# A recurrence and a routed expert layer: loads of two steps at a time

## The chip, the cores and the metric

The kernel runs on one core of one Trainium2 chip. Its engines are TensorE (PE, with its weight load PEld), VectorE (DVE), ScalarE (ACT), GpSimd (POOL) and SyncE (SP), which issues nearly all transfers. The metric is the device time of one execution in microseconds. The kernel before takes 266.89 us, the median of 3 runs (266.56 to 266.95).

## The reference

Attention with a decaying state over 4 batches, 8 heads, 768 positions and heads of 48, and behind it a layer of 8 experts, each row going to one of them.

```python
for t in range(S):
    kt, vt, rt = (k[:, :, t], v[:, :, t], r[:, :, t])
    cur = np.einsum('bhd,bhe->bhde', u[None] * kt, vt)
    y[:, :, t] = np.einsum('bhd,bhde->bhe', rt, state + cur)
    state = w[None, :, :, None] * state + np.einsum('bhd,bhe->bhde', kt, vt)
...
x = y.transpose(0, 2, 1, 3).reshape(B * S, H * D)
do_compute = x @ w_skip > 0
e_idx = argmax(x @ w_gate);  gate_w = softmax(x @ w_gate)[e_idx]
out = x + gate_w * (relu(x @ w1[e_idx]) @ w2[e_idx])   # rows with do_compute, else out = x
```

All is float32. The experts' weights are split into two parts on the chip, a high and a low one, and each product is made of three.

## The kernel before

**Stage 1, the recurrence (to about 113 us).** The 768 positions are cut into 12 steps of 64 (`NSTEP`), and two batches are handled together, so there are 24 steps in all (`NT`, two runs of 12). For step n the kernel loads one block `dm` with r and k (128 partitions, 4 KB each: two heads' 48 channels in rows 0 to 47 and 64 to 111; the other 32 rows are zeros in memory, loaded with the rest) and one block `vz` with v (positions in the partitions; two batches in two halves, each loaded by its own transfer of 64 rows; the rest of the tile is set to zero once, L323). Then

- `prep_r` (DVE, L418 and L426, with ACT L412) multiplies r by powers of the decay into `rd`; `prep_k` (POOL, L436; DVE for step 0) does k into `kd`.
- `scores` (PE, L448) multiplies `kd` by `rd` into `ps_p`; `mask_scores` (DVE, L469, L470) copies the valid part into `am`.
- `turn_k` (PE L461, ACT L463) transposes `kd`; `state` (PE, L481) multiplies it by v.
- `within` (PE, L510: `am` by v) and `across` (PE, L534: `rd` by the state so far) give the output in `ps_y`; `evac` (ACT, L545) copies it to `xt`, and SP stores it (L563, two transfers, three for steps 4 to 7).
- Every four steps the gate's scores are made and routed (L605, L622, the lines of `route`).

The loop at L902 runs n from 0 to 22. Its iteration n makes `scores(n+1)`, `turn_k(n+2)`, `prep_k(n+3)`, `prep_r(n+3)`, `state(n+1)` and `within(n+1)`, ends with the store of step n+1, and on SP issues `load_dm(n+5)`, `load_v(n+4)` and, in 15 of the iterations, a piece of the weights (`raw`, L110, 256 KB). The written order is the order on each engine: nothing is scheduled. SP's transfers stand in one queue; each waits besides its data for the transfer eight places before it to have landed. `dm` has four buffers, and so has `vz`; `load_dm(n+5)` writes into the buffer of step n+1, when `rd` and `kd` of that step are made.

**Stage 2 (to about 131 us)** finishes the routing, gathers the first rows (POOL, L128) and starts the first expert with the rows transposed; its tiles `xhl`, `h` (tag `dm`) take buffers of the pool `ld`. **Stage 3** runs the other experts, PE-bound matmuls on gathered rows, weights loaded by SP and split by ACT, DVE and POOL.

Of the kernel before, what the change touches and what calls it, by code (L numbers as in the profile page):

```python
# [9 lines left out]
F32 = mybir.dt.float32  # L10
# [10 lines left out]
B, H, S, D = 4, 8, 768, 48  # L21
N, DM, E, F = B * S, H * D, 8, 1024
P = 128
C = 64
# [4 lines left out]
NHP = H // 2  # L29
NT = NPAIR * NSTEP  # L30
# [8 lines left out]
DR = P  # L39
ADV = NB * NHP  # L40
BIG = 4 * N
NVK = 4
GB = 4
BH = 2
NDM = 4
# [16 lines left out]
def tile_wkv_moe(  # L62
# [11 lines left out]
    nc = tc.nc  # L74
# [168 lines left out]
        mix(y, q)  # L243


    lctx = ExitStack()
    ld = lctx.enter_context(tc.tile_pool(name="ld", bufs=NDM, side="right"))
    vctx = ExitStack()
    vp = vctx.enter_context(tc.tile_pool(name="vp", bufs=1, side="right"))
    with ExitStack() as actx:  # L250
# [17 lines left out]
        ub_sb = tab.tile([DR, NHP], F32, name="ub_sb")  # L268
        nc.scalar.dma_start(out=ub_sb, in_=ub)

        loaded = {}
        vz = [vp.tile([P, 2, 2, NHP, D], F32, name=f"vz{j}") for j in range(NVK)]

        def load_dm(n):
            pr, i = divmod(n, NSTEP)
            d = ld.tile([P, 2, NHP, 2, C], F32, tag="dm", name=f"dm{n}", bufs=NDM)
            nc.sync.dma_start(out=d, in_=dm[pr, i])
            loaded[n] = [d[:DR], None]

        def load_v(n):  # L280
            pr, i = divmod(n, NSTEP)
            t = vz[n % NVK]
            for q in range(2):
                half = slice(q * C, (q + 1) * C)
                nc.sync.dma_start(out=t[half, q], in_=tok[pr, i, half])
            loaded[n][1] = t

        load_dm(0)
        load_dm(1)
        load_v(0)  # L290
        load_dm(2)
        load_v(1)
        load_dm(3)
        load_v(2)
        load_v(3)
        wgp = tab.tile([P, NCC, 2, C // 2], F32, name="wgp")
        pick = tab.tile([P, 2, NB, E + 1], F32, name="pick")

# [21 lines left out]
        eye = lower("eye", ALU.is_equal)  # L320
        for t in vz:
            for q in range(2):
                nc.gpsimd.memset(t[(1 - q) * C : (2 - q) * C, q], 0.0)  # L323

        w_d = tab.tile([DR, NSUB, 2, NHP, C], F32, name="w_d")

# [85 lines left out]
                nc.scalar.mul(rd[:, :, 1], rd[:, :, 0], uw[:, hp : hp + 1])  # L412

        def prep_r(n, parts=(0, 1)):
            d = loaded[n][0]
            if 0 in parts:
                rds[n] = wk.tile([DR, NHP, 2, 2, C], F32, tag="rd", name=f"rd{n}", bufs=4)
                nc.vector.tensor_tensor(  # L418
                    rds[n][:, :, :, 0],
                    d[:, 0],  # L420
                    w_d[:, n % NSUB, 0][:, :, None].to_broadcast([DR, NHP, 2, C]),
                    ALU.mult,
                )
            if 1 in parts:
                rd = rds[n]
                nc.vector.tensor_tensor(  # L426
                    rd[:, :BH, :, 1],
                    rd[:, :BH, :, 0],
                    (uw if n < 3 else uw_p)[:, :BH, None, None].to_broadcast([DR, BH, 2, C]),
                    ALU.mult,  # L430
                )

        def prep_k(n, eng=None):
            d = loaded[n][0]
            kds[n] = wk.tile([DR, NHP, 2, C], F32, tag="kd", name=f"kd{n}", bufs=4)
            (eng or nc.gpsimd).tensor_tensor(  # L436
                kds[n],
                d[:, 1],
                w_d[:, n % NSUB, 1][:, :, None].to_broadcast([DR, NHP, 2, C]),
                ALU.mult,  # L440
            )
# [28 lines left out]
            nc.vector.copy_predicated(shape(am[n % 2]), eye, p[:, :, 1])  # L470

        def state(n):
            t = loaded[n][1]
            i, sub = n % NSTEP, n % NSUB
            if i == NSTEP - 1:
                return
            kt = kts.pop(n)
            s, nxt = ps_s[:, : 2 * NHP * D].rearrange("p (q f) -> p q f", q=2), sblk[(n + 1) % 2]
            for hp in range(NHP):
                for a in range(2):  # L480
                    nc.tensor.matmul(  # L481
                        s[a * C : (a + 1) * C, :, hp * D : (hp + 1) * D],
                        kt[:, hp, a, :],
                        t[:, :, a, hp, :],
                        start=i == 0 and hp == 0,
                        stop=True,
                        skip_group_check=True,
                    )
            if sub < NSUB - 1:
                nc.scalar.copy(nxt, s)  # L490
                return
            heads = lambda t: t.rearrange("p q (h e) -> p q h e", h=NHP)
            nc.vector.tensor_tensor(
                heads(nxt), heads(s), wh_sb[:, None, :, None].to_broadcast([P, NB, NHP, D]), ALU.mult
            )
            return lambda: nc.scalar.copy(s, nxt)
# [5 lines left out]
        def place_y(a, c):  # L502
            return ps_y[c * C : (c + 1) * C, a, : NHP * D].rearrange("p (q g e) -> p q g e", q=NB, g=NHP // 2)

        def within(n, behind=None):
            t = loaded[n][1]
            for g in range(NHP // 2):
                for a, c in FOUR:
                    hp = 2 * g + (a ^ c)
                    ins = nc.tensor.matmul(  # L510
                        place_y(a, c)[:, :, g, :],
                        am[n % 2][:, a, hp * C : (hp + 1) * C],
                        t[:, :, a, hp, :],
                        start=g == 0 and n % NSTEP == 0,
                        stop=True,
                        skip_group_check=True,
                    )
                    if behind is not None:
                        tc.add_manual_dep(
                            ins.ins,  # L520
                            behind.name,
                            mybir.DependencyInfo(mybir.DependencyClass.Sync, mybir.DependencyReason.DATA),
                            reason="other row tiles write these banks",
                        )
                        behind = None
# [320 lines left out]
            return banks[kind][(used[kind] - 1) % len(banks[kind])]  # L846

        def scratch(name, shape, dt, tag):
            return (ld if tag == "dm" else scr[0]).tile(
                [P] + shape, dt, tag=tag, name=name, bufs=NDM if tag == "dm" else 3  # L850
            )

        scr = []
# [14 lines left out]
        def piece(j, split=False):  # L868
            e, j = divmod(j, NPC)
            if split:  # L870
                split_piece(e, j, nc.gpsimd)
            else:
                load_piece(e, j)

        setup = setup_routes()
        prep_r(0)
        bonus(0, BH)
        prep_k(0, nc.vector)
# [14 lines left out]
        warm(1)  # L893
        within(0)
        evac(0)
        load_v(4)
        nc.sync.dma_start(out=wgp, in_=wgq)
        prep_r(2)
        bonus(2, BH)
        prep_k(2)  # L900
        grow(3)
        for n in range(NT - 1):  # L902
            if n + 5 < NT:
                load_dm(n + 5)
            if n + 4 < NT and n:
                load_v(n + 4)
            if n in LOADS:
                piece(LOADS.index(n))
            scores(n + 1)
# [37 lines left out]
        done = NPC  # L947
        piece(len(LOADS))
        vctx.close()
        scr.append(lctx.enter_context(tc.tile_pool(name="scr", bufs=3, side="right", reuse_waits="tile")))  # L950
        first = begin(0, "dm")

# [378 lines left out]
```

## Time and profile before

| | |
|---|---|
| median of the runs | 266.89 us (266.56 to 266.95) |
| profiled execution, whole | 264.4 us |
| its span | 262.6 us |
| granted TensorE clock | 0.996 |
| PE busy | 247.9 us, 94% |
| DVE, ACT, POOL busy | 181.0, 140.5, 131.7 us |
| moved by transfers | 53.92 MB, mean 205 GB/s |

The span is what the profiler saw from the first to the last instruction; around it the execution needs 1.8 us more. The runs without a profile lie 2.5 us above the profiled execution. PE's busy time is matmuls in a pipeline with ends that are modelled, so it tells where PE had nothing to do and not how full it was. A wait in the profile is put down to the one of several releasers that came last.

### The profile page before, as it was taken

The page shows a single profiled execution, that of the slowest core. Times are in us where ns is not written, and L with a number is a line of the kernel's source. Part 1 is how long each engine was busy: PE and PEld are TensorE (multiplying, and loading weights), DVE is VectorE, ACT ScalarE, POOL GpSimd, SP SyncE. Part 2 cuts the span into 40 slices and gives each one's busy share as a digit, 9 for nine tenths or more (in the row PEclk, how much of TensorE's full clock was granted, in tenths as well). Part 3 has the DMA queues.
Part 4 walks back from the last instruction along what each step waited for, and adds up shares of the span by engine and source line. Part 5 has one row for each costly group of instructions (what it writes and reads, how often), then busy time and mean ns, then how long its engine had stood idle before and what let it go on. Part 6 is the DMA issues. An engine that isn't in the chain of part 4 may idle for free.

```text
span 262.6 us, 8820 instructions
## 1 busy us (share of the span) xinstructions
PE 247.9 (94%) x3594; PEld 228.5 (87%) x3594; DVE 181.0 (69%) x366; ACT 140.5 (53%) x314; POOL 131.7 (50%) x130
## 2 busy tenths in 40 slices
PE   7799999989999999998999999999999999999990
PEld 2698898977988989877899899999999999999980
DVE  7976667786888989674567997979277484692210
ACT  2555667757865767434658628358085381660200
POOL 8656424547555365405689818454535355345011
PEclk9999999999999999999999999999999999999998
DMA  6978779899987897767798896877648475001000
GB/s 195 268 225 253 216 223 272 264 255 269 273 256 226 257 245 243 204 189 243 222 308 261 267 325 206 261 238 244 215 143 255 141 228 199 20 1 47 1 34 21
DMA packets 31137, 53.92 MB, mean 205 GB/s; under 512 B 4603, under 2 KB 14471, under 8 KB 31088
## 3 DMA queue, kind: packets, MB, share of 16 engines
q1 hardware_dynamic: 28896, 48.09, 60.5%
q0 software_dynamic: 2048, 5.18, 6.5%
q8 instruction: 30, 0.49, 0.8%
q14 instruction: 19, 0.16, 0.2%
q10 hardware_dynamic: 144, 0.00, 0.0%
HBM read 45.46 MB, written 8.39 MB: 205 GB/s over the span
## 4 chain that ended last, share of the span: by engine, by line
PE 82%; DMA 5%; DVE 4%; ACT 2%; POOL 2%; issue 1%; SPq 0%; POOLq 0%; DVEq 0%; ACTq 0%
PE ps_y L170 11%; PE ps_p L170 10%; PE ps_p L448 7%; PE ps_y L510 6%; PE ps_s L481 6%; PE ps_p L160 5%; PE ps_r L160 5%; PE ps_l L160 5%; PE ps_y L160 5%; PE ps_l L461 4%; PE ps_y L534 3%; PE ps_t L577 3%; PE ps_l L605 2%; POOL kd L436 2%; DMA xg<-out_dram,gid 2%; DMA raw<-in_w_dram 2%
## 5 line engine op out<-in xcount | busy, mean ns | idle before, releaser
L116 POOL TENSOR_TENSOR lo<-raw,hi 128x512 fp32r<-128x512 f32 x40 | 52.8, 1324 | 39.8 <-ACT hi L115 39.6
L115 ACT CAST hi<-raw 128x512 fp32r<-128x512 f32 x96 | 54.7, 623 | 1.9 <-DMA raw<-in_w_dram 1.7
L116 DVE TENSOR_TENSOR lo<-raw,hi 128x512 fp32r<-128x512 f32 x56 | 51.1, 936 | 2.5 <-ACT hi L115 2.3
L436 POOL TENSOR_TENSOR kd<-dm,w_d 128x512 f32<-128x512 f32 x23 | 33.6, 1460 | 31.5 <-DMA dm<-in_dm_dram 14.5
L178 POOL DMA_INDIRECT out_dram<-xg,sid x16 | 17.4, 1084 | 37.6 <-DVE xg L175 29.1
L469 DVE COPY_PREDICATED am<-below,ps_p 128x512 f32<-128x512 int8 x24 | 17.7, 736 | 13.4 <-PE ps_p L448 13.2
L448 PE MATMUL ps_p<-rd,kd 64*64 64x128 f32 x768 | 26.7, 276 | 0.0
L128 POOL DMA_INDIRECT xg<-out_dram,gid x16 | 18.5, 1153 | 15.3 <-DMA raw<-in_w_dram 10.6
L164 ACT ACTIVATE hh<-ps_p 128x464 fp32r<-128x464 f32 x7 | 3.9, 559 | 37.7 <-PE ps_p L160 35.7
L418 DVE TENSOR_TENSOR rd<-dm,w_d 128x512 f32<-128x512 f32 x24 | 21.9, 912 | 3.1 <-DMA dm<-in_dm_dram 3.1
L448 PEld LDWEIGHTS ps_p<-rd,kd 64*64 64x64 f32 x768 | 20.9, 133 | 3.3 <-issue 1.2
L510 PE MATMUL ps_y<-vz,am 128*64 128x96 f32 x384 | 20.3, 248 | 0.9 <-DVE am L470 0.7
L463 ACT COPY kt<-ps_l 128x512 f32<-128x512 f32 x22 | 12.9, 585 | 14.2 <-PE ps_l L461 13.9
L412 ACT ACTIVATE rd<-rd,uw 128x128 f32<-128x128 f32 x50 | 17.2, 394 | 6.0 <-DVE rd L418 5.6
L170 PE MATMUL ps_p<-hi,hh 128*128 128x384 f32 x56 | 19.4, 347 | 0.0
L170 PE MATMUL ps_p<-hi,hl 128*128 128x384 f32 x56 | 19.0, 340 | 0.4 <-DVE hl L165 0.4
L481 PE MATMUL ps_s<-vz,kt 128*64 128x96 f32 x352 | 19.4, 253 | 0.0
L170 PE MATMUL ps_y<-hi,hh 128*104 128x384 f32 x56 | 18.9, 338 | 0.0
L510 PEld LDWEIGHTS ps_y<-vz,am 128*64 128x64 f32 x384 | 17.2, 137 | 1.9 <-DVE am L470 1.1
L170 PE MATMUL ps_y<-hi,hl 128*104 128x384 f32 x56 | 18.9, 337 | 0.0
L170 PE MATMUL ps_y<-lo,hh 128*104 128x384 f32 x56 | 18.9, 337 | 0.0
L170 PE MATMUL ps_p<-lo,hh 128*128 128x384 f32 x56 | 18.8, 336 | 0.0
(252 smaller groups left out, 653.1 us busy)
## 6 DMA issues: line engine op xcount, KB each, us to landing
raw<-in_w_dram SPq DMA_DIRECT2D x96, 256.0 KB, 4.0
dm<-in_dm_dram SPq DMA_DIRECT2D x24, 512.0 KB, 5.4
vz<-in_tok_dram SPq DMA_DIRECT2D x48, 96.0 KB, 4.8
out_dram<-xt SPq DMA_DIRECT2D x48, 96.0 KB, 4.1
out_dram<-xt SPq DMA_DIRECT2D x4, 192.0 KB, 4.3
xg<-out_dram,gid POOLq DMA_INDIRECT x16, 4.8
out_dram<-xg,sid POOLq DMA_INDIRECT x16, 3.7
wgp<-in_wgq_dram SPq DMA_DIRECT2D x1, 96.0 KB, 2.1
```

The source lines that it names most:

```text
L115: nc.scalar.copy(hi, t)
L116: eng.tensor_tensor(lo, t, hi.bitcast(F32), ALU.subtract)
L128: ins = nc.gpsimd.indirect_dma_start(out=xg[:m], out_offset=None, in_=out[0:rows], in_offset=bass.IndirectOffsetOnAxis(ap=gid[:m, q : q + ...
L160: nc.tensor.matmul(ph, a[:, c, fs], b[:, c, :], start=(k == 0), stop=(k == 3 * NCC - 1))
L170: nc.tensor.matmul(py, a, b[:, f, :], start=(k == 0), stop=(k == 3 * NFC - 1))
L178: ins = nc.gpsimd.indirect_dma_start(out=out, out_offset=bass.IndirectOffsetOnAxis(ap=sid[: listed(q), q : q + 1], axis=0), in_=xs.pop(q)[ ...
L418: nc.vector.tensor_tensor(rds[n][:, :, :, 0], d[:, 0], w_d[:, n % NSUB, 0][:, :, None].to_broadcast([DR, NHP, 2, C]), ALU.mult,)
L436: (eng or nc.gpsimd).tensor_tensor(kds[n], d[:, 1], w_d[:, n % NSUB, 1][:, :, None].to_broadcast([DR, NHP, 2, C]), ALU.mult,)
L448: nc.tensor.matmul(ps_p[q * C : (q + 1) * C, a, 2 * hp * C : 2 * (hp + 1) * C], kd[h, hp, q, :], rd[h, hp, q].rearrange("p s c -> p (s c)" ...
L469: nc.vector.copy_predicated(shape(am[n % 2]), below, p[:, :, 0])
L481: nc.tensor.matmul(s[a * C : (a + 1) * C, :, hp * D : (hp + 1) * D], kt[:, hp, a, :], t[:, :, a, hp, :], start=i == 0 and hp == 0, stop=Tr ...
L510: ins = nc.tensor.matmul(place_y(a, c)[:, :, g, :], am[n % 2][:, a, hp * C : (hp + 1) * C], t[:, :, a, hp, :], start=g == 0 and n % NSTEP ...
```

## The change

`dm` lives in two lasting tiles of two steps each, `vz` too. Steps 0 to 3 load all 128 rows, one step at a time, step 0 by two transfers (r, then k). From step 4 on, `load_dm` is called in every second iteration and loads two steps by two transfers, one of rows 0 to 47 and one of rows 64 to 111; the zeros of the first loads stay in the other rows. `load_v` loads two steps by two transfers, one for each half. With that, a pair is written when both of its steps have been used. In iteration n (odd) it is `load_dm(n+5)` with steps n+5 and n+6, and `load_v(n+3)` with n+3 and n+4. The pool `ld` is closed with `vp` at the end of stage 1, and the tiles of stage 2 with the tag `dm` come from the pool that had the others.

```diff
-        loaded = {}
-        vz = [vp.tile([P, 2, 2, NHP, D], F32, name=f"vz{j}") for j in range(NVK)]
+        loaded, steps_v = {}, {}
+        vz = [vp.tile([P, 2, 2, 2, NHP, D], F32, name=f"vz{j}") for j in range(NVK // 2)]
+
+        dmz = [ld.tile([P, 2, 2, NHP, 2, C], F32, name=f"dmz{j}") for j in range(NDM // 2)]

         def load_dm(n):
             pr, i = divmod(n, NSTEP)
-            d = ld.tile([P, 2, NHP, 2, C], F32, tag="dm", name=f"dm{n}", bufs=NDM)
-            nc.sync.dma_start(out=d, in_=dm[pr, i])
-            loaded[n] = [d[:DR], None]
+            d = dmz[n % NDM // 2]
+            if n < NDM:
+                for s in (0, 1) if n == 0 else (slice(0, 2),):
+                    nc.sync.dma_start(out=d[:, n % 2, s], in_=dm[pr, i, :, s])
+                loaded[n] = d[:, n % 2]
+                return
+            for h in range(2):
+                rows = slice(h * C, h * C + D)
+                nc.sync.dma_start(
+                    out=d[rows].rearrange("p i s h q c -> p i (s h q c)"),
+                    in_=dm[pr, i : i + 2, rows].rearrange("i p s h q c -> p i (s h q c)"),
+                )
+            for j in range(2):
+                loaded[n + j] = d[:, j]

         def load_v(n):
             pr, i = divmod(n, NSTEP)
-            t = vz[n % NVK]
+            t = vz[n % NVK // 2]
             for q in range(2):
                 half = slice(q * C, (q + 1) * C)
-                nc.sync.dma_start(out=t[half, q], in_=tok[pr, i, half])
-            loaded[n][1] = t
+                nc.sync.dma_start(out=t[half, :, q], in_=tok[pr, i : i + 2, half].rearrange("i p a h d -> p i a h d"))
+            for j in range(2):
+                steps_v[n + j] = t[:, j]

         load_dm(0)
         load_dm(1)
         load_v(0)
         load_dm(2)
-        load_v(1)
         load_dm(3)
         load_v(2)
-        load_v(3)
...
-        load_v(4)
         nc.sync.dma_start(out=wgp, in_=wgq)
...
         for n in range(NT - 1):
-            if n + 5 < NT:
+            if n % 2 and n + 5 < NT:
                 load_dm(n + 5)
-            if n + 4 < NT and n:
-                load_v(n + 4)
+            if n % 2 and n + 3 < NT:
+                load_v(n + 3)
...
         vctx.close()
+        dctx.close()
```

How the transfers stand on SP, in three places. First the front of the program. A row names the tile that is written (with its number), what is read, the partitions and the elements of each, and what is waited for (DMAHW: an earlier transfer of this queue). Before:

```order
L267 DMA w_in_123<-in_wd_dram 128x16
L277 DMA dm0_131<-in_dm_dram 128x1024
L277 DMA dm1_133<-in_dm_dram 128x1024
L285 DMA vz0_127<-in_tok_dram 64x384 x2
L277 DMA dm2_137<-in_dm_dram 128x1024
L285 DMA vz1_128<-in_tok_dram 64x384
L285 DMA vz1_128<-in_tok_dram 64x384 [waits DMAHW0_49]
L277 DMA dm3_141<-in_dm_dram 128x1024 [waits DMAHW1_49]
```

and now:

```order
L267 DMA w_in_123<-in_wd_dram 128x16
L281 DMA dmz0_129<-in_dm_dram 128x512 x2
L281 DMA dmz0_129<-in_dm_dram 128x1024
L298 DMA vz0_127<-in_tok_dram 64x2x384 x2
L281 DMA dmz1_130<-in_dm_dram 128x1024
L281 DMA dmz1_130<-in_dm_dram 128x1024 [waits DMAHW0_49]
L298 DMA vz1_128<-in_tok_dram 64x2x384 [waits DMAHW1_49]
L298 DMA vz1_128<-in_tok_dram 64x2x384 [waits DMAHW2_49]
L286 DMA dmz0_129<-in_dm_dram 48x2x1024 [waits DMAHW3_49,DMAHW4_49,DVE_49,Pool_49]
```

Step 0 has become two transfers, v of step 1 has moved ahead of dm of step 2, and the load of steps 4 and 5 waits for DVE and POOL, which make rd and kd of steps 0 and 1.

The second place is the middle of stage 1, from the store of step 9 to the next. Before:

```order
L563 DMA out_0_dram<-xt9_1040 64x2x192 [waits DMAHW6_49]
L277 DMA dm14_1044<-in_dm_dram 128x1024 [waits DMAHW7_49,DVE_49,Pool_49]
L285 DMA vz1_128<-in_tok_dram 64x384 [waits DMAHW0_49,PE_49]
L285 DMA vz1_128<-in_tok_dram 64x384 [waits DMAHW1_49]
L110 DMA raw0_4_1048<-in_w12_dram 128x512 [waits DMAHW2_49]
L563 DMA out_0_dram<-xt10_1119 64x2x192 [waits DMAHW3_49,Activation_49]
L563 DMA out_0_dram<-xt10_1119 64x2x192 [waits DMAHW4_49]
L277 DMA dm15_1123<-in_dm_dram 128x1024 [waits DMAHW5_49,DVE_49,Pool_49]
L285 DMA vz2_129<-in_tok_dram 64x384 [waits DMAHW6_49,PE_49]
L285 DMA vz2_129<-in_tok_dram 64x384 [waits DMAHW7_49]
L110 DMA raw0_5_1127<-in_w12_dram 128x512 [waits DMAHW0_49]
```

and now:

```order
L575 DMA out_0_dram<-xt9_1009 64x2x192 [waits DMAHW1_49]
L286 DMA dmz1_130<-in_dm_dram 48x2x1024 [waits DMAHW2_49,DVE_49,Pool_49]
L286 DMA dmz1_130<-in_dm_dram 48x2x1024 [waits DMAHW3_49]
L298 DMA vz0_127<-in_tok_dram 64x2x384 [waits DMAHW4_49,PE_49]
L298 DMA vz0_127<-in_tok_dram 64x2x384 [waits DMAHW5_49]
L110 DMA raw0_4_1017<-in_w12_dram 128x512 [waits DMAHW6_49]
L575 DMA out_0_dram<-xt10_1088 64x2x192 [waits DMAHW7_49,Activation_49]
L575 DMA out_0_dram<-xt10_1088 64x2x192 [waits DMAHW0_49]
L110 DMA raw0_5_1092<-in_w12_dram 128x512 [waits DMAHW1_49]
```

Two iterations had two transfers of dm and four of v between their stores; now iteration 9 has two of dm and two of v, and iteration 10 has none.

The third place is DVE in step 0. Before:

```order
L358 TENSOR_TENSOR uw_187<-ub_sb_125,pw_122 128x4 [waits DMAHW0_49]
L418 TENSOR_TENSOR rd0_201<-dm0_131,w_d_170 128x8x64 [waits DMAHW2_49,DVE_49]
L426 TENSOR_TENSOR rd0_201<-rd0_201,uw_187 128x4x64 [waits DVE_49]
L436 TENSOR_TENSOR kd0_206<-dm0_131,w_d_170 128x512
L329 TENSOR_TENSOR w_d_170<-w_d_170,pw_122 128x512
```

and now:

```order
L370 TENSOR_TENSOR uw_176<-ub_sb_125,pw_122 128x4 [waits DMAHW0_49]
L430 TENSOR_TENSOR rd0_190<-dmz0_129,w_d_159 128x8x64 [waits DMAHW2_49,DVE_49]
L438 TENSOR_TENSOR rd0_190<-rd0_190,uw_176 128x4x64 [waits DVE_49]
L448 TENSOR_TENSOR kd0_195<-dmz0_129,w_d_159 128x512 [waits DMAHW3_49]
L341 TENSOR_TENSOR w_d_159<-w_d_159,pw_122 128x512
```

rd waits for the first transfer (r) and kd for the second (k), where both waited for one.

More of the change, by code (lines that the diff above doesn't have):

```diff
@@ L243, in single @@
         mix(y, q)
-    lctx = ExitStack()
-    ld = lctx.enter_context(tc.tile_pool(name="ld", bufs=NDM, side="right"))
+    lctx, dctx = ExitStack(), ExitStack()
+    ld = dctx.enter_context(tc.tile_pool(name="ld", bufs=1, side="right"))
     vctx = ExitStack()
@@ L322, in tile_wkv_moe @@
             for q in range(2):
-                nc.gpsimd.memset(t[(1 - q) * C : (2 - q) * C, q], 0.0)
+                nc.gpsimd.memset(t[(1 - q) * C : (2 - q) * C, :, q], 0.0)
         w_d = tab.tile([DR, NSUB, 2, NHP, C], F32, name="w_d")
@@ L414, in prep_r @@
         def prep_r(n, parts=(0, 1)):
-            d = loaded[n][0]
+            d = loaded[n]
             if 0 in parts:
@@ L433, in prep_k @@
         def prep_k(n, eng=None):
-            d = loaded[n][0]
+            d = loaded[n]
             kds[n] = wk.tile([DR, NHP, 2, C], F32, tag="kd", name=f"kd{n}", bufs=4)
@@ L472, in state @@
         def state(n):
-            t = loaded[n][1]
+            t = steps_v[n]
             i, sub = n % NSTEP, n % NSUB
@@ L505, in within @@
         def within(n, behind=None):
-            t = loaded[n][1]
+            t = steps_v[n]
             for g in range(NHP // 2):
@@ L848, in scratch @@
         def scratch(name, shape, dt, tag):
-            return (ld if tag == "dm" else scr[0]).tile(
+            return scr[0].tile(
                 [P] + shape, dt, tag=tag, name=name, bufs=NDM if tag == "dm" else 3
```

## The prediction

> **What bounds the kernel now.** I read the page's head, then who TensorE (PE) waits for, in its own stretch, the recurrence (7 to 113 us), and then the transfers behind those waits.
>
> ```profile
> span 262.6 us, 8820 instructions
> PE 247.9 (94%) x3594; PEld 228.5 (87%) x3594; DVE 181.0 (69%) x366; ACT 140.5 (53%) x314; POOL 131.7 (50%) x130
> ...
> PE 82%; DMA 5%; DVE 4%; ACT 2%; POOL 2%; issue 1%; SPq 0%; POOLq 0%; DVEq 0%; ACTq 0%
> ```
> ```profile
> PE ps_l L461 <- POOL kd L436: 1.6, 3, 0.9
> PE ps_l L461 <- DVE kd L436: 0.9, 1, 0.9
> PE ps_y L510 <- DVE am L470: 0.7, 1, 0.7
> PE ps_y L534 <- issue: 0.6, 1, 0.6
> ```
> The last four rows are waits: who waited for whom, us in total, times, the longest. PE is 94% busy, and the chain of waits is 82% PE, so the change can win only PE's gaps. In the recurrence they are 3.8 us in these rows: 1.6 for the k product kd of POOL (three times), 0.9 + 0.7 in the first step, and 0.6 that nothing explains.
>
> Why kd is late shows in the timeline. Round n is iteration n of L902; it opens with `scores(n+1)` (PE L448). Counted from the front, the dm issue at 52.05 is step 13's, which the program puts in round 8.
>
> ```profile
> 50.04 1.03 PE ps_p L448 x32
> ```
> ```profile
> 50.60 1.34 SPq L563 DMA_DIRECT2D out_dram<-xt  x2
> 52.05 0.55 SPq L277 DMA_DIRECT2D dm<-in_dm_dram  x1
> 52.69 1.15 SPq L285 DMA_DIRECT2D vz<-in_tok_dram  x2
> 53.89 1.06 SPq L110 DMA_DIRECT2D raw<-in_w_dram  x1
> 55.05 1.34 SPq L563 DMA_DIRECT2D out_dram<-xt  x2
> 57.69 1.10 PE L448 MATMUL ps_p<-rd,kd 64*64 64x128 f32 x32
> 57.86 0.48 ACT L545 COPY xt<-ps_y 128x384 f32<-128x384 f32 x1 [0.65 <-PE ps_y L510]
> 57.90 1.73 POOL L436 TENSOR_TENSOR kd<-dm,w_d 128x512 f32<-128x512 f32 x1 [2.41 <-PE ps_y L510]
> 59.64 0.75 DVE L470 COPY_PREDICATED am<-eye,ps_p 128x512 f32<-128x512 int8 x1
> 59.69 0.66 PE L461 MATMUL ps_l<-ident,kd 128*128 128x128 f32 x4 [0.89 <-POOL kd L436]
> 60.61 0.88 PE L481 MATMUL ps_s<-vz,kt 128*64 128x96 f32 x16
> ```
> ```profile
> dm<-in_dm_dram SPq DMA_DIRECT2D x24, 512.0 KB, 5.4
> vz<-in_tok_dram SPq DMA_DIRECT2D x48, 96.0 KB, 4.8
> wgp<-in_wgq_dram SPq DMA_DIRECT2D x1, 96.0 KB, 2.1
> ```
> ```profile
> 45.00:62.00 17.00, 15.70 (x401) 13.63 (x397) 12.28 (x30) 11.53 (x29) 9.46 (x7) 1.00 0.91 265
> 79.00:96.00 17.00, 16.67 (x429) 14.95 (x425) 14.65 (x34) 11.10 (x29) 8.98 (x7) 1.00 0.83 243
> ```
> At 50.04 PE opens round 9, and SP is only coming to round 8's load: its issues stand end to end (1.34, 0.55, 1.15, 1.06 = 4.1 us a round, with 0.1 between), so it runs a round behind. With the median 5.4, step 13 lands near 57.5. POOL starts kd at 57.90; the PE row named there ended long before in the sense of the data, so I read the releaser as the transfer. PE wants kd at 58.80 and gets it at 59.63: the 0.89. The last two fences are the transfers (us from issue to landing at the end) and two stretches of time (busy time and count of PE, weight load, DVE, ACT, POOL; then clock, share of the engines that move data, GB/s). Those engines are 0.83 to 0.91 busy; 265 GB/s at 0.91 makes 291 GB/s when full. So two things are short in the recurrence, SP's issue time and the transfer engines, and they reach PE three times.
>
> **The change, part by part.**
>
> *Fewer issues.* For two steps, SP issued 2 dm + 4 vz + 4 stores and some 1.3 weight pieces, 11.3; now 2 + 2 + 4 + 1.3 = 9.3. At 0.55 to 0.67 each, 1.2 us in two rounds come free, and SP catches up.
>
> *Fewer bytes.* A dm row block of 512 KB becomes 96 of 128 rows, 384 KB. v, stores and weights stay. For two steps 1024 + 384 + 384 + 330 = 2.1 MB become 1.87 MB, 12% less; the share of 0.91 would be 0.80.
>
> *Step 13 again.* It now comes with step 12, issued in round 7:
>
> ```profile
> 41.33 1.03 PE ps_p L448 x32
> ```
> ACT has copied a result out 0.65 after a round opens (57.69 to 58.34), three stores at 0.67 take 2.0, so the pair is issued from about 44.0. Landing is the 5.4 above plus 256 KB more at 291 GB/s (0.9) = 6.3: 50.3. POOL needs 1.3 to 1.7 for kd, so it must land by 57.1 for PE at 58.80. Slack 6.8 us where it was -0.9; with the longest dm landing below, 7.4, still 4.8. A pair's first step has the shorter lead, its second a round more. The three waits go: **-1.6**. What is late next is the mask: L470 ends at 60.39, and without the wait PE would come to L510 at about 60.4. So I let 0.14 come back, which is what such a place costs today:
>
> ```profile
> 91.75 0.88 PE L481 MATMUL ps_s<-vz,kt 128*64 128x96 f32 x16
> 91.88 0.75 DVE L470 COPY_PREDICATED am<-eye,ps_p 128x512 f32<-128x512 int8 x1
> 92.78 0.88 PE L510 MATMUL ps_y<-vz,am 128*64 128x96 f32 x16
> ```
> Bounds of this part: -1.6 and 0.
>
> *The wait that is added.* The pair overwrites both of its steps, so SP waits for the second one's kd and rd, made one round before. Behind it on SP stand v, a weight piece and the next stores. Even as late as kd is in the rows above, it ends 1.94 us after its round opens (57.69 to 59.63); SP comes to the pair 0.65 + 1.34 = 2.0 after, and data that come earlier make kd earlier. Cost nothing; what this wait takes beyond 2.0 it takes from v's slack below.
>
> *v.* The pair (n+3, n+4) is issued in odd round n, after the dm pair, one round nearer to its use than before. In round 9: stores done at 51.95, dm issues until 53.1, v until 54.3. Data start some 2.1 after an issue with nothing queued (the wgp row, its own 0.3 in it); 768 + 384 KB take 4.05 at 291 GB/s, so v lands at 51.95 + 2.1 + 4.05 = 58.1. PE needs it at L481 of round 11: 60.61 less the 0.89, 59.7. Slack 1.6 us; PE would wait directly if that is used up. Cost 0; upper bound below, with the rivals.
>
> *The front.* r of step 0 is now a transfer of its own, and by the order above rd waits for that one alone; that the split would do nothing can be left out as far as the program goes.
>
> ```profile
> 1.26 3.98 DMA dm<-in_dm_dram
> ```
> ```profile
> 4.78 0.15 DVE L358 TENSOR_TENSOR uw<-ub_sb,pw 128x4 f32<-128x4 f32 x1
> 5.35 0.69 DVE L418 TENSOR_TENSOR rd<-dm,w_d 128x512 f32<-128x512 f32 x1 [0.41 <-DMA dm<-in_dm_dram]
> 6.42 0.69 DVE L436 TENSOR_TENSOR kd<-dm,w_d 128x512 f32<-128x512 f32 x1
> 7.25 0.63 PE L461 MATMUL ps_l<-ident,kd 128*128 128x128 f32 x4 [0.92 <-DVE kd L436]
> 11.08 1.46 DVE L418 TENSOR_TENSOR rd<-dm,w_d 128x512 f32<-128x512 f32 x1
> ```
> Half the bytes land 0.9 earlier, at 4.35; DVE is busy with its table until 4.93. So at most 0.41 is won, k is there at 5.3 for kd at 6.0, and one more SP issue (0.45) hides behind data already queued. Step 1's v now precedes dm of step 2: 192 KB, 0.65, so that dm lands about 10.7 where rd of step 2 would like it at 10.67. I take **-0.35** (bounds -0.41 and 0).
>
> Sum: -1.6 + 0.14 - 0.35 = **-1.8 us**. The profiled execution took 264.4 us with a span of 262.6, so a span of 260.8; the runs' median is 266.89, 2.5 above it, and I take the same difference there: **265.1 us**. Stages behind 113 us are carried along: their order is unchanged, and new tiles stand where dm and v stood, written after PE's L510 of the last step.
>
> [...] The trace's half loads are vz: 64 rows, landing in 2.5 at best, against 2.1 for wgp with the same 96 KB on all rows.
>
> ```profile
> DMA to landing us min/median/max: 2.5/4.8/7.0
> ...
> DMA to landing us min/median/max: 3.6/5.4/7.4
> ```
> (First vz, then dm.) [...]
>
> **Rivals.**
>
> *v comes late* (slower). Place: L481 of every even-step `state` after a pair. By the two rows above, a half costs up to 0.4 per 96 KB: 8 x 0.4 = 3.2 for the dm pair. It decides from 1.6 on. At the bound v is 1.6 late, ten times, 16 us; at two thirds of it (2.1) 0.5 late, 5 us: 266.9 - 1.9 + 5 = 270. For it: the bursts of pairs, and the wait for kd in front of v on the same queue. Against: vz is moved by halves today, at 0.83 to 0.91 share and 243 to 265 GB/s, with no sign that rounds with many halves are slower. 14%.
>
> *The wait only changes its name* (same). DVE is busy 14.65 of 17 us in 79 to 96, and rd stretches from 0.69 to 1.46 when it runs beside POOL's kd, which earlier data make more frequent. PE would then wait for masks where it waited for kd; only the front remains: 266.5. Against it: DVE itself waits for PE's scores in most rounds.
>
> ```profile
> DVE am L469 <- PE ps_p L448: 13.2, 12, 2.1
> ```
> 16%.
>
> *More than the rows show.* The 0.6 wait without a cause (PE L534) also goes with lighter queues, and nothing comes back: 266.9 - 0.4 - 1.6 - 0.6 = 264.3. 12%.
>
> *Forecast*, 265.1: 58%; its own range 264.6 to 266.0.
>
> **How the numbers follow.** About 0.2%, 0.53 us, can be told from no change. Faster: most of the forecast (0.54), the large gain (0.12) and a little of the renamed wait (0.02), 0.68. Same: 0.14 + 0.04 = 0.18. Slower 0.14. The range, 263.9 to 267.2, leaves out the late v and a small tail below.
>
> **What would show it.** Right: PE's row L461 <- POOL kd gone or under 0.3; the first rd at 4.95 to 5.0; DMA share between 45 and 62 near 0.8; SP with idle time before its stores; dm landing one round or more before kd. Wrong: a row PE ps_s (`state`) <- DMA vz (v late), or PE ps_y L510 <- DVE am growing by what kd lost (renamed), or dm pairs landing over 8 us after their issue.

## The result and the profile after

The changed kernel takes **289.0 us** (286.8 to 291.9), the kernel before 266.9: the ratio is **1.086** with an interval of 1.077 to 1.096. Forecast were 265.1 us and a range up to 267.2. It is slower by 22 us where a gain of 1.8 was worked out. All ratios here leave disturbed runs out; of e1, e9 and e15 below two runs each are left.

Lines have moved by 12 from the recurrence on (`scores` L460, `turn_k` L473, `state` L493, `within` L522, `across` L546, dm loads L281 and L286, v L298). The head of the page after, with PE's clock, the share of the transfer engines and GB/s in 40 slices:

```profile
span 288.5 us, 8773 instructions
PE 258.6 (90%) x3594; PEld 237.4 (82%) x3594; DVE 179.0 (62%) x366; ACT 140.0 (49%) x314; POOL 129.4 (45%) x126
PEclk9899979797999977999999999999999999999997
DMA  6979969899799765954678979848865847200000
GB/s 181 239 156 190 165 173 167 248 194 191 178 211 203 163 149 109 239 141 116 181 233 251 317 212 317 282 157 296 257 208 165 264 131 247 88 1 26 17 32 21
PE 77%; DMA 11%; issue 5%; DVE 2%; ACT 1%; SPq 1%; POOL 0%; POOLq 0%; DVEq 0%
```

The span grew by 25.9. PE is busy 10.7 longer (258.6 against 247.9) and idle 15.2 longer (29.9 against 14.7). The loss lies in the recurrence: but for the last slice, those with a clock under 9 are in the first half, and there the rate is mostly under 200 GB/s, where it was mostly over 200 before. The first products on gathered rows, in PE's timeline before and after, come 25.5 us later, so nearly all of it lies ahead of them:

```profile
124.84 0.55 PE L151 MATMUL ps_t<-ident,xg 128*128 128x128 f32 x3 [1.05 <-DMA xg<-out_dram,gid]
```
```profile
150.37 0.55 PE L151 MATMUL ps_t<-ident,xg 128*128 128x128 f32 x3 [1.23 <-DMA xg<-out_dram,gid]
```

The time has gone to three things. The first is the transfers, in stretches (us of the span; busy time and count of PE, weight load, DVE, ACT, POOL; then clock, share, GB/s):

```profile
45.00:62.00 17.00, 14.63 (x343) 12.96 (x341) 7.62 (x17) 9.11 (x23) 5.04 (x4) 0.90 0.98 201
96.00:112.00 16.00, 12.83 (x242) 11.61 (x241) 8.25 (x20) 6.85 (x18) 6.43 (x6) 0.79 0.63 127
```

Before, 45 to 62 read 265 GB/s at a share of 0.91. Now it reads 201 at 0.98: the engines are full and move a quarter less. (The share is the sum of the packets' times over that of 16 engines, so it can read a little over 1.) The second is who PE waits for:

```profile
PE ps_p L460 <- issue: 4.0, 2, 2.4
PE ps_s L493 <- issue: 3.2, 2, 2.8
PE ps_y L546 <- issue: 2.9, 2, 1.5
PE ps_r L802 <- issue: 2.5, 1, 2.5
PE ps_s L493 <- ACT rd L424: 2.4, 1, 2.4
PE ps_s L493 <- DMA vz<-in_tok_dram: 2.1, 2, 1.5
PE ps_t L589 <- issue: 1.2, 1, 1.2
```

Waits for kd are gone from the list, as forecast, and v is there, as the first rival had it. But the largest part, 13.8 us in the five rows of "issue", is time in which PE waited for nothing that the profile shows; before, this was one stall of 0.6. The third is the clock. One such stall in the timeline of PE, and the same place in stretches:

```profile
35.36 0.46 PE L493 MATMUL ps_s<-vz,kt 128*64 128x96 f32 x5
38.65 0.63 PE L493 MATMUL ps_s<-vz,kt 128*64 128x96 f32 x10 [2.83 <-issue]
40.41 1.99 PE L460 MATMUL ps_p<-rd,kd 64*64 64x128 f32 x32
```
```profile
32.50:35.80 3.30, 3.30 (x94) 2.71 (x82) 1.81 (x3) 1.79 (x7) 0.00 (x0) 1.00 1.03 152
35.80:38.60 2.80, 0.02 (x1) 0.00 (x0) 0.65 (x2) 0.22 (x1) 1.43 (x2) 1.00 1.07 266
40.40:42.40 2.00, 2.00 (x45) 1.99 (x46) 0.00 (x0) 1.07 (x3) 0.00 (x0) 0.50 0.25 91
```

PE stops in the middle of one `state`, after five of its equal products, with kt and vz in place, while the transfer engines are full (1.07). Within 2 us of starting again its clock is 0.50, and the 32 products of `scores` take 1.99 where they took 1.10 at full clock. The mean clock of the execution fell from 0.996 to 0.959; 247.9 x 0.996 / 0.959 = 257.5, so by this estimate the clock is about 9.6 of the 10.7 us of longer PE time. The trace bears it out: up to 112 us the clock stands at 0.50 in five stretches (from 12.1, 39.4, 53.1 and 66.7 for 3.4 us each, from 104.3 for 6.8), 20.5 us in all, and PE is busy in nearly all of them. The first follows the wait for rd (2.4), the others stand behind or in four of the stalls without a releaser.

### The profile page after: what moved, and what is told of

The parts are those of the page before. It is cut to its first block, busy times and chain, and to the rows that moved or that the text cites. A ratio compares the mean times of both kernels' runs of the same rounds, so it can differ in the third digit from the quotient of the medians.

```text
span 288.5 us, 8773 instructions
## 1 busy us (share of the span) xinstructions
PE 258.6 (90%) x3594; PEld 237.4 (82%) x3594; DVE 179.0 (62%) x366; ACT 140.0 (49%) x314; POOL 129.4 (45%) x126
## 2 busy tenths in 40 slices
DMA packets 30257, 51.30 MB, mean 178 GB/s; under 512 B 4235, under 2 KB 14103, under 8 KB 30208
## 4 chain that ended last, share of the span: by engine, by line
PE 77%; DMA 11%; issue 5%; DVE 2%; ACT 1%; SPq 1%; POOL 0%; POOLq 0%; DVEq 0%
PE ps_p L170 10%; PE ps_y L170 10%; PE ps_p L460 7%; PE ps_y L522 6%; PE ps_s L493 6%; DMA vz<-in_tok_dram 5%; PE ps_p L160 5%; PE ps_r L160 5%; PE ps_l L160 5%; PE ps_y L160 5%; PE ps_l L473 3%; PE ps_y L546 3%; PE ps_t L589 2%; DMA dmz<-in_dm_dram 2%; PE ps_l L617 2%
## 5 line engine op out<-in xcount | busy, mean ns | idle before, releaser
L116 DVE TENSOR_TENSOR lo<-raw,hi 128x512 fp32r<-128x512 f32 x56 | 51.7, 948 | 2.5 <-ACT hi L115 2.2
L448 POOL TENSOR_TENSOR kd<-dmz,w_d 128x512 f32<-128x512 f32 x23 | 31.1, 1357 | 16.3 <-DMA dmz<-in_dm_dram 16.3
L178 POOL DMA_INDIRECT out_dram<-xg,sid x16 | 18.3, 1143 | 37.3 <-DVE xg L175 25.6
L460 PE MATMUL ps_p<-rd,kd 64*64 64x128 f32 x768 | 30.8, 298 | 4.0 <-issue 4.0
L460 PEld LDWEIGHTS ps_p<-rd,kd 64*64 64x64 f32 x768 | 24.0, 146 | 8.4 <-issue 6.5
L493 PE MATMUL ps_s<-vz,kt 128*64 128x96 f32 x352 | 21.1, 262 | 7.7 <-issue 3.2
L493 PEld LDWEIGHTS ps_s<-vz,kt 128*64 128x64 f32 x352 | 16.6, 143 | 11.6 <-issue 6.4
L475 ACT COPY kt<-ps_l 128x512 f32<-128x512 f32 x22 | 12.9, 586 | 25.9 <-PE ps_l L473 25.8
L522 PE MATMUL ps_y<-vz,am 128*64 128x96 f32 x384 | 22.8, 265 | 0.1
L522 PEld LDWEIGHTS ps_y<-vz,am 128*64 128x64 f32 x384 | 19.6, 150 | 1.1 <-issue 0.6
L424 ACT ACTIVATE rd<-rd,uw 128x128 f32<-128x128 f32 x50 | 17.2, 395 | 5.1 <-DVE rd L430 5.1
L430 DVE TENSOR_TENSOR rd<-dmz,w_d 128x512 f32<-128x512 f32 x24 | 17.4, 725 | 2.4 <-DMA dmz<-in_dm_dram 2.4
```

Source lines behind the costliest of these rows:

```text
L116: eng.tensor_tensor(lo, t, hi.bitcast(F32), ALU.subtract)
L178: ins = nc.gpsimd.indirect_dma_start(out=out, out_offset=bass.IndirectOffsetOnAxis(ap=sid[: listed(q), q : q + 1], axis=0), in_=xs.pop(q)[ ...
L430: nc.vector.tensor_tensor(rds[n][:, :, :, 0], d[:, 0], w_d[:, n % NSUB, 0][:, :, None].to_broadcast([DR, NHP, 2, C]), ALU.mult,)
L448: (eng or nc.gpsimd).tensor_tensor(kds[n], d[:, 1], w_d[:, n % NSUB, 1][:, :, None].to_broadcast([DR, NHP, 2, C]), ALU.mult,)
L460: nc.tensor.matmul(ps_p[q * C : (q + 1) * C, a, 2 * hp * C : 2 * (hp + 1) * C], kd[h, hp, q, :], rd[h, hp, q].rearrange("p s c -> p (s c)" ...
L493: nc.tensor.matmul(s[a * C : (a + 1) * C, :, hp * D : (hp + 1) * D], kt[:, hp, a, :], t[:, :, a, hp, :], start=i == 0 and hp == 0, stop=Tr ...
```

## The experiments

Theory A: a transfer into rows of one half of the partitions moves slower per byte. Theory B: two steps loaded at once are a burst, and v, r of step 1 and PE's own program (in the trace the queue q8, "instruction", with 30 packets of 16 KB spread over the span) come late behind it. Theory C: v by pairs is the cause; theory D: lasting tiles, the split of step 0, or SP's wait for both steps. Losses below are the ratio to the kernel before, in per cent. "Issue" is the sum of PE's waits of that name up to 113 us of the profiled execution. e3, e4 and e19 are single runs, against 267.4, 267.4 and 268.4. e1's profile is of its longest run (281.5; the others 276.3 to 281.3), so its 9.2 may be high; every "issue" is of one execution.

| | r and k | v | loss | issue, us |
|---|---|---|---|---|
| before | 128 rows, single | single | 0 | 0.6 |
| e5 | 128 rows, single | single | -0.15 (-0.55 to 0.26) | 1.3 |
| e6 | 128 rows, single | pairs | 1.6 (0.8 to 2.3) | 2.1 |
| e11 | 128 rows, pairs of two transfers | single | 1.4 (0.7 to 2.0) | 1.8 |
| e9 | 128 rows, pairs of two transfers | pairs | about 2.3 | 5.8 |
| e1 | 128 rows, pairs of one transfer | pairs | 3.9 (2.9 to 5.0) | 9.2 |
| e4 | 48 rows, single | single | 2.8 | none |
| e3 | 48 rows, pairs | single | 3.7 | 9.3 |
| e18 | 48 rows, pairs, halves in turn | pairs | 1.9 (0.9 to 2.9) | 2.4 |
| the change | 48 rows, pairs | pairs | 8.6 (7.7 to 9.6) | 13.8 |
| e2 | 64 rows, pairs | pairs | 8.4 (7.7 to 9.1) | 17.2 |

### Parts of the change, one by one

**Lasting tiles and the split of step 0 alone (e5).** `load_dm` loads one step in all rows, v as before.

```diff
-            for h in range(2):
-                rows = slice(h * C, h * C + D)
-                nc.sync.dma_start(out=d[rows]..., in_=dm[pr, i : i + 2, rows]...)
+            nc.sync.dma_start(out=d[:, n % 2], in_=dm[pr, i])
```

> All loads one step at a time, r and k in all 128 rows, issued in the rounds of the kernel before; only the lasting tiles and the two transfers of step 0 are left of the change. If pairs (bursts) and half rows are the whole cause: 266.3 to 267.3, the kernel before less the 0.35 of the front, PE's rows with 'issue' at most 0.6 as before. If the lasting tiles or the split cost something of their own: above 268.

Measured: 0.9985 (0.9945 to 1.0026). Theory D falls for tiles and split: they cost nothing that shows. The first rd, from the timeline of DVE in e5:

```profile
4.94 0.69 DVE L425 TENSOR_TENSOR rd<-dmz,w_d 128x512 f32<-128x512 f32 x1
```

It starts at 4.94 where it started at 5.35: the 0.41 that the prediction had as its bound for the front.

**v by pairs alone (e6), and r and k by pairs alone (e11).** e6 is e5 with the change's `load_v`; e11 is e5 with both steps' loads issued in the odd round.

```diff
+            for j in range(2):                      # e11
+                nc.sync.dma_start(out=d[:, j], in_=dm[pr, i + j])
```

> Only v comes in pairs; r and k as before, one step at a time and all 128 rows, though in the lasting tiles and with step 0 by two transfers. Theory A: v went into half the partitions before too, so 265.5 to 267.5. Theory C (v by pairs comes late): above 272, with PE waiting for vz.

> The same transfers as the kernel with singles (512 KB for a step, v singly), but those of two steps are issued back to back in every second round: only the time of issue differs. Theory B (a burst holds up what is queued behind it, PE's program blocks among it): 270 to 275, PE rows with 'issue' 3 us or more in all. If a burst only hurts together with v by pairs or with half rows: 266.3 to 267.5, 'issue' under 1.

Measured: e6 1.0155 (1.0082 to 1.0228), between what the two theories gave. e11 1.0137 (1.0072 to 1.0201), 270.5 us, at the low end of theory B, but its "issue" is 1.8 and not 3 or more. A burst of whole rows costs, and as far as its one profile shows, little of it is PE's program. In e6 most of it is one place, the first step:

```profile
PE ps_s L487 <- ACT rd L418: 3.3, 1, 3.3
PE ps_p L454 <- issue: 1.0, 2, 0.5
PE ps_y L516 <- issue: 0.8, 2, 0.4
```

Two steps of v are now under way beside r and k of step 1; rd of step 1 comes late and PE waits 3.3 us. The other runs with v by pairs have 2.1 to 3.3 there (e9 0.9), put down to rd or to vz; those with v singly at most 1.1.

**Half rows alone (e4), and the change without pairs of v (e3).** e4 issues two transfers of 48 rows for one step; e3 is the change with `load_v` of before.

> The change with r and k one step at a time (each step by two transfers of 48 rows, 192 KB each) and v one step at a time; nothing comes in pairs, SP waits for one step only. Theory A: same rows, so 275 to 289 us, about 200 GB/s at full share. Theory B (bursts) and theory D (SP's wait for both steps of a pair): 265 to 268.

> The change, with v loaded as in the kernel before (one step at a time, 4 x 96 KB in two rounds). Theory A: the 48-row transfers of r and k are all still there, so 280 to 289 us and about 200 GB/s at full share. Theory C (v by pairs is late, since it is issued a round nearer to its use): the waits for vz go and the time is back at 265 to 268.

Measured: e4 274.9, just under what theory A gave and well above B's; e3 277.2, likewise under A's 280 and above C's. So no part alone is the change: half rows, pairs and v by pairs each cost 1.4 to 2.8% (the 2.8 from a single run), and together 8.6. In e4 PE has no "issue" in its rows, but kd again:

```profile
PE ps_l L470 <- POOL kd L445: 4.5, 5, 1.3
PE ps_y L519 <- ACT xT L587: 2.9, 2, 1.7
```

SP has 13.3 issues in two rounds there in place of 11.3, so this run does not price the rows alone. Its clock is 0.981 without a stall of "issue"; e3, with 9.3 us of them and none over 2.0, kept 0.997. So the clock does not simply follow these stalls.

### Which rows, and in what turn

**All 128 rows, one transfer of 1 MB (e1); 64 rows (e2); 48 rows in turn (e18).** The edits to the loop over halves:

```diff
-            for h in range(2):
-                rows = slice(h * C, h * C + D)
+            for rows in (slice(0, P),):                       # e1
+            for rows in (slice(0, C), slice(C, P)):           # e2
+            for j in range(2):                                # e18: four transfers,
+                for h in range(2):                            # one half of one step each
```

> The change with one edit: the pair of r and k is loaded by one transfer of all 128 rows (1 MB) in place of two of 48 rows (2 x 384 KB). Pairs, lasting tiles, the wait of SP for both steps, v by pairs and the split of step 0 stay. Theory A (a transfer into rows of one half of the partitions moves slower per byte, so the transfer engines are full at some 200 GB/s and v and the program's own blocks come late): back near the kernel before, 265 to 268 us, GB/s above 240 where the share is 0.9, PE's rows with 'issue' under 2 us in all, granted clock above 0.98. Theory B (pairs come in bursts, and a burst holds up what is queued behind it whatever its rows are): bursts are a third larger here, so 289 us or more, with the same issue gaps.

> The change with its two transfers of a pair taking rows 0 to 63 and 64 to 127 (512 KB each) in place of 0 to 47 and 64 to 111 (384 KB): the bytes of the kernel before, in halves. [...] If a half goes at a fixed rate of some 200 GB/s: a third more bytes in dm, longer than the change, 294 to 305 us. [...] If 48 rows are the odd number that is slow: as with whole rows in one transfer, 277 to 282.

> The change with each pair loaded by four transfers of 48 rows and 192 KB, in the order first half and second half of one step, then of the other; same bytes, same rounds, two issues more in two rounds. If a half is slow because the other half's way in stands idle meanwhile, turns of 192 KB in place of 384 KB let the two overlap at each change: 230 to 290 GB/s where r and k move alone (177 to 203 in the change), the time 276 to 284. If transfers of 48 rows are slow as such: 180 to 205 GB/s there and 287 to 292.

Stretches in which r and k make up nearly all packets; kernel before, the change, e1, e2, e18, in this order, columns as above:

```profile
85.50:86.50 1.00, 1.00 (x56) 0.94 (x51) 0.96 (x3) 1.00 (x4) 0.00 (x0) 1.00 0.88 335
94.50:95.50 1.00, 1.00 (x44) 0.95 (x37) 0.74 (x1) 1.00 (x4) 0.30 (x1) 1.00 0.96 370
```
```profile
44.50:48.50 4.00, 4.00 (x111) 3.66 (x109) 2.33 (x5) 2.64 (x7) 0.00 (x0) 1.00 1.04 178
66.00:69.50 3.50, 3.50 (x54) 3.14 (x56) 1.02 (x2) 2.10 (x6) 1.76 (x2) 0.60 0.96 200
```
```profile
83.50:86.00 2.50, 2.50 (x94) 2.38 (x88) 2.42 (x5) 2.06 (x6) 1.25 (x1) 1.00 0.90 342
106.00:108.50 2.50, 2.50 (x91) 2.33 (x87) 2.29 (x9) 1.53 (x5) 0.96 (x1) 1.00 0.99 366
```
```profile
55.50:59.50 4.00, 4.00 (x115) 3.46 (x113) 1.50 (x3) 2.87 (x8) 1.72 (x2) 1.00 1.07 236
65.00:69.50 4.50, 4.50 (x89) 3.96 (x88) 0.51 (x2) 2.06 (x6) 1.23 (x1) 0.67 1.05 216
```
```profile
61.00:64.00 3.00, 3.00 (x70) 2.78 (x71) 0.22 (x1) 1.16 (x4) 0.00 (x0) 0.54 1.03 219
87.00:90.00 3.00, 3.00 (x109) 2.68 (x105) 1.52 (x4) 2.22 (x6) 0.58 (x2) 1.00 1.00 254
```

Over all such stretches, whole rows move at 299 to 370 GB/s in singles (four, two of them at a share of only 0.79 and 0.83) and at 295 to 366 in the pairs of e1 (six, mean 332). 64 rows of one half move at 216 to 236, 48 rows at 178 to 200 (six stretches each). So a pair of 768 KB at about 188 holds the engines 4.2 us, and e2's 1 MB at about 225 holds them 4.7; e1's 1 MB, at 332, only 3.2. The change moves fewer bytes than whole rows and takes longer. Theory A is right on the rate, and e2 adds that leaving the zeros out of a half saves little: a quarter of the bytes, 0.5 of 4.7 us, and nothing of the time (289.0 us in both, for e2 between its two readings; 1.084 and 1.086).

e1 takes 280.6 us, between theory A's 268 and theory B's 289, and still loses 3.9%: the rate is not all, and the rest goes with pairs, r and k or v, as in theory B. e18 has the bytes and the rows of the change and two issues more, and takes **272.8 us**, 1.019 (1.009 to 1.029), better than expected. Its rate rises only to 219 to 254; what falls most is "issue", from 13.8 to 2.4. It still waits for v (2.3 of the 7.0 in the first step):

```profile
PE ps_s L491 <- DMA vz<-in_tok_dram: 7.0, 4, 2.4
PE ps_p L458 <- issue: 2.1, 1, 2.1
```

**One transfer cut in two (e9).** e1 with two transfers of 512 KB.

> The run with pairs of whole rows in one transfer of 1 MB (280.6, PE waits with 'issue' 8.8 us in all), with one edit: two transfers of 512 KB, one for each step, back to back. Same bytes, same rows, same burst, v by pairs as there. So far the waits for PE's program are long where one transfer lasts 2 us or more (48 rows 2.0, 64 rows 2.3, 1 MB 3.2 us by its bytes and rate) and short where it lasts 1.6 or less (whole singles 1.6, in turn 0.8). Theory L (what counts is how long one transfer stands on its engines): 'issue' at most 3.5 us in all, 272 to 275. Theory B (the burst as a whole counts): 'issue' 7 to 10 and 278 to 282 as before.

Measured: 271.6 and 272.1 us, against 264.3 to 268.2 before: at the low end of theory L. "Issue" fell from 9.2 to 5.8, in the gap between the two theories (3.5 and 7). That cutting a transfer helps is likely from e18 and e9 together and not shown by e9 alone: it and e1 have two runs each and no interval between them. Some of the burst's cost is left; e11, the same without pairs of v, has an "issue" of 1.8. How the two share it is not settled.

**Two queues (e12, e15).** ScalarE issues the second half, at the same place (e12) or between `bonus` and `turn_k` (e15). In e15 the rows 64 to 111 of steps 4 and 5 aren't loaded and keep older data.

```diff
-                nc.sync.dma_start(
+                (nc.sync, nc.scalar)[h].dma_start(
```

> The change with the second half of each pair (rows 64 to 111) issued by ScalarE on its own queue, at the same place of the round, so that both halves of the partitions are written at once; bytes, pairs and v as in the change. Theory A by halves (each half has its own way in, and one alone is slow): GB/s at full share rises from 200 toward 260 to 290, and the time falls from 289 to between 272 and 283, the bursts being left. If 48-row transfers are slow as such, or if the transfer engines are the limit: about 200 GB/s and 286 to 292.

> As the run with the halves on two queues, but ScalarE issues its half one to two microseconds later in the round, so that it moves beside SyncE's half and not ahead of it. If one half alone is slow because the other half's way in stands idle: where both halves of a pair are under way GB/s rises to 250 or more at full share, and the time falls under the 279.4 of the two queues one after the other, to 271 to 277. If transfers of 48 rows are slow whatever runs beside them: 278 to 282 and 200 GB/s.

Measured: e12 1.036 (1.028 to 1.044), e15 about 1.06 (280.6 and 281.2 us). Neither tells what it was made for. In e12 ScalarE issued its half 1.8 us ahead of SyncE, in e15 still up to 2.3, so one half had mostly moved when the other began. Rows of the timeline, first of e12 and then of e15:

```profile
29.03 0.32 ACTq L286 DMA_DIRECT2D dmz<-in_dm_dram  x1
30.80 0.53 SPq L286 DMA_DIRECT2D dmz<-in_dm_dram  x1
```
```profile
38.44 0.32 ACTq L286 DMA_DIRECT2D dmz<-in_dm_dram  x1
40.69 0.54 SPq L286 DMA_DIRECT2D dmz<-in_dm_dram  x1
```

A stretch of e12 in which ScalarE's half moves alone, at 191 GB/s:

```profile
30.00:32.00 2.00, 2.00 (x53) 1.78 (x46) 1.97 (x3) 1.39 (x4) 1.31 (x2) 1.00 0.96 191
```

So whether both halves at the same moment would reach the rate of whole rows was not seen; e18's 219 to 254 is the only sign of an overlap. Why e12 is 10 us shorter than the change is open; its "issue" is 10.5.

### PE's program

**The program shifted (e19).** Eight of fifteen warming products are replaced by 40 small ones, so that every later instruction of PE stands 64 further on.

```diff
-        warm(NWARM)
+        warm(7)
+        for _ in range(40):
+            nc.tensor.matmul(ps_t[:32, :32], ones[:, :32], ones[:, :32], start=True, stop=True)
```

> The change with PE's program shifted by 64 instructions: eight of the fifteen warming products before the first scores are replaced by 40 small ones; nothing else moves. In the change eight of the stalls without a releaser stand before PE's instruction 194 or 195 of a block of 256, counted from its first. Theory F (PE waits for the next block of its program, which is fetched through the transfer engines): they stand at 194 or 195 again by count, which is 64 instructions earlier in the work, so at other lines. If they belong to the work at their places: the same lines as in the change, count 2 or 3. The time is 285 to 292 under both.

Counted from PE's first instruction in the trace (matmuls and weight loads), the change's stalls stand before number 1219, 1731, 2242, 2498, 3011, 3267, 3522, 3778: each 194 or 195 above a multiple of 256. In e19 they stand before 961, 1217, 3522, 3778 and 4545, again 193 or 194 above one, though the work there is another. The waits of e19:

```profile
PE ps_y L548 <- issue: 11.5, 4, 4.7
PE ps_s L495 <- DMA vz<-in_tok_dram: 5.2, 3, 2.6
PE ps_s L495 <- ACT rd L426: 2.3, 1, 2.3
PE ps_y L524 <- issue: 0.8, 2, 0.5
```

Four lines had stalls of more than a microsecond in the change besides `across`; here only `across` (L548) has. The stalls go with the count and not with the work: theory F holds. The queue q8 of the trace ("instruction", 30 packets of 16 KB) stands in the page among the queues of the sixteen engines that move the loads:

```profile
q8 instruction: 30, 0.49, 0.8%
```

The packets' own times in the trace close the argument. Each of the eight stalls of the change ends 1.3 to 1.7 us after a packet of this queue has ended (the one of 2.83 us at 38.65, the packet at 37.36); so does the 0.56 of the kernel before (at 22.07, the packet at 20.72). From one of the eight to the next, one packet ends where the counts lie 255 or 256 apart and two where they lie 511 to 513 apart. So a packet goes with 256 of PE's instructions here, and by these times PE goes on when its packet has come.

In the kernel before one such wait shows, of 0.6 us; under the change's loads they take up to 2.8 us, and 4.7 in e19.

### The front, fewer rows, and the load ahead of the stores

**The front as before (e17).** v of the first four steps singly, in the order of before; the rest is the change.

> The change with v of the first four steps loaded one step at a time in the order of the kernel before; from step 4 on all as in the change. The first scores waited 2.4 us for r of step 1, which landed 1.4 later behind a double v. If the front's price is that wait alone: 289 - 2.4 = 286 to 287. If the low clock after it (0.92 from 7 to 28 us) belongs to it too: 283 to 286. The rest, 17 us or more over the kernel before, is of the rounds behind it.

Measured: 1.076 (1.070 to 1.083). In its profile (of its longest run) the 2.4 us wait of the first step is gone, and the loss is 7.6% where it was 8.6, with intervals that overlap: the front is at most a small part. By the ratio it is 287.3 us, just above the 286 to 287 expected for that wait alone.

**112 rows, single (e8).** e5 with rows 0 to 111 in one transfer.

> As the kernel with singles in lasting tiles, and each step of r and k from step 4 on by one transfer of rows 0 to 111 (448 KB in place of 512; the rows 48 to 63 go along as zeros). It saves half of the bytes that the change saved, without a burst and with no transfer that lies in one half of the partitions alone. If half rows and bursts are the causes: 2 x 64 KB less for two steps are 0.44 us at 291 GB/s, each step lands 0.2 earlier, the waits L461 <- kd of 1.6 fall to about 1.0: 265.5 to 266.7, 4096-byte rows at the same rate as in the kernel before. If leaving rows out is itself what slows a transfer: GB/s at full share falls to about 200 and the time is above 270.

Measured: 1.0032 (0.9993 to 1.0071). Fewer bytes, whole span of partitions, no burst, and still nothing won. In 45 to 62 it moves 253 GB/s at 0.91, where the kernel before had 265; the stretch mixes all transfers, so it does not give the rate of this one:

```profile
45.00:62.00 17.00, 14.79 (x383) 12.88 (x373) 12.23 (x28) 11.21 (x28) 9.11 (x7) 1.00 0.91 253
```

**r and k ahead of the stores (e16).** e5 with `load_dm(n + 6)` written ahead of `evac(n + 1)`.

> Singles in lasting tiles (no pairs, no half rows), with each step's r and k issued by SyncE ahead of the stores of the round before, 1.3 us or more earlier, the stores 0.55 later. This is the prediction's step 13 without its price: if kd is late because SyncE comes late to the load, the waits L461 <- kd (1.6 in all) go and nothing else moves: 0.35 + 1.2 to 1.6 less than before, 264.9 to 265.7. If the waits for kd have another cause, or what is won comes back at the masks: 266 to 267.

Measured: 265.0 us against 266.1 beside it, 0.9978 (0.9937 to 1.0018): by the ratio 0.6 us less, where 1.6 to 2.0 had been expected, and not to be told from no change. In its profile the waits of PE for kd are 0.5, from 1.6 in the kernel before, and nothing has come in their place. But e5, which lacks this one edit, has only 0.7. First e16, then e5:

```profile
PE ps_l L468 <- POOL kd L443: 0.5, 2, 0.3
PE ps_y L517 <- DVE am L477: 0.4, 1, 0.4
```
```profile
PE ps_l L468 <- POOL kd L443: 0.7, 2, 0.4
```

So this run does not show by itself why kd was late. What the edit moved is POOL's wait for r and k, 19.8 us in e5 and 7.2 in e16: the data come earlier when SyncE issues them earlier, which fits the prediction's reading, and PE hardly gains by it. This kernel is the fastest seen, by a span of 260.9 against 262.6, but no interval shows it faster.

## Why the prediction was wrong, point by point

- **What bounds the kernel.** Right as far as it went: SyncE's issue time and the transfer engines. That "the change can win only PE's gaps" was true, and left out how much it can lose where the engines are 0.8 to 0.9 busy.
- **Fewer issues.** Right. In the change SyncE has nothing to issue from 34.98 to 41.04 (PE stands still for 2.8 us of it). It won no time.
- **Fewer bytes.** This step failed. The bytes came out as forecast (51.30 MB after 53.92, 128 KB in each of 20 steps). The share did not: 0.98 and not 0.80, since the 291 GB/s of before was taken for transfers that reach into one half. It measures 178 to 200 there.
- **Step 13 again.** The three waits went, as forecast; that they were owed to SyncE's late issue fits but was not isolated (e5 has 0.7 of them without it, e16 0.5 with it). The 0.14 let back in for the mask does not follow from its rows, by which PE would come to L510 at 60.6, after the mask's end at 60.39; nothing hangs on it. A pair takes 4.2 us of the engines and not 2.7 (768 KB at 291 GB/s).
- **The added wait.** Not separated: e11 has it together with the burst, for 1.4% in all.
- **v.** Called free with 1.6 us of slack. It is late: 2.1 us of PE waits in the change, 7.0 in e18 (2.3 of them in the first step), where the rest is better.
- **The front.** rd of step 0 came at 5.00, as forecast, for 0.35. The sentence that the extra load "hides" failed: v by pairs put rd of step 1 late by 2.4 (3.3 in e6). e17 puts its price near 1% of the time, with overlapping intervals.
- **The half loads of the trace.** From the landings of vz and wgp (2.5 and 2.1) the first rival had up to 3.2 us more for a pair of r and k, and 2.1 at the two thirds that it took: 4.8 us in place of 2.7; 4.2 was measured. That was near the mark and was carried only to v, as a rival of 270 us with 14%. Put in place of 2.7 into the term "fewer bytes", the 4.8 and the other 1.1 MB at 291 GB/s make 8.7 us for two rounds, which took 8.7 (41.33 to 50.04): engines that are full, and the question would have been who else needs them.
- **The rivals.** "v comes late" had the right place and sign; 270 was far too little. "The wait only changes its name" did not happen: no row of PE waiting for am stands in the list. "More than the rows show" fell: the 0.6 without a cause grew to 13.8.
- **What was not in it at all.** 13.8 us for PE's own program behind the loads, and some 10 us for the lower clock, which mostly came with such stalls. The row "PE ps_y L534 <- issue: 0.6" stood in the prediction as a wait that nothing explains; by count it stands before PE's number 707, 195 above a multiple of 256. It was the same wait, in small: it ends 1.35 us after a packet of the queue q8 has ended.

## What to carry to other kernels

Bytes were the wrong measure here where a transfer reached only one half of the partitions (178 to 236 GB/s in pairs by halves, and 295 to 370 for whole rows): look for a stretch of the trace that moves such a transfer alone, and use its GB/s; leaving out the zero rows of a half won no time here. Where the transfer engines are as busy as here (0.83 to 0.91 before the change), ask what else goes through them, PE's program included, and try the same bytes in shorter transfers in turn, which took 272.8 us here and not 289.0. A PE wait with no releaser is worth counting: here such waits stood a multiple of 256 apart in the instruction stream, and it was the program that was late.

## What had not been expected of the hardware

- Stalls of 0.4 to 4.7 us before PE instructions whose number lies 193 to 195 above a multiple of 256 (eight in the change, with the transfer engines at a share of 1.02 to 1.08 during six of them and of 0.61 and 0.52 during two; five in e19), and a clock of 0.50 within 2 us of four of the change's. That the stall brings the clock down was seen in order of time, not tested by itself, and the stalls of 1.2 to 1.6 at 72.8, 85.4 and 91.3 brought none.
- The same 768 KB in four transfers in turn in place of two: 272.8 us and not 289, "issue" 2.4 and not 13.8.
- Taking 16 rows out of a transfer (e8) won nothing: 1.0032, with 253 GB/s at a share of 0.91 against 265.
